# Load order, wave order, dummy matmuls and a wider handover at the start of an attention block

## The chip, the cores and the metric

The kernel runs on one core of one Trainium2 chip. The metric is the time of one execution on the device in microseconds (us). The profile gives the span from the first to the last instruction on the core; it reads about 1.7 us less than the timed figure (863.2 against 864.9 for the same execution of the kernel before).

## The reference

Two residual blocks follow each other. In both, layernorm comes first and has no learned scale.

```python
# x: 2048 x 1024, H = 32 heads of 32
qkv = layernorm(x) @ wqkv                # 1024 -> 3 x 1024
pq, pk = phi(q), phi(k)                  # phi(t) = (t + 1 if t > 0 else exp(t)) + 1e-6
kv = einsum("bhsd,bhse->bhde", pk, v)    # summed over all 2048 tokens
z  = einsum("bhsd->bhd", pk)
o  = (pq @ kv) / (pq . z + 1e-6)
h  = x + o @ wo
gate, up = layernorm(h) @ W_gate, layernorm(h) @ W_up   # 1024 -> 3584
out = h + (relu(gate) * up) @ W_down                    # 3584 -> 1024
```

`kv` and `z` need all tokens, so K and V are made for all 2048 tokens before the first output of the attention can be made. Q needs only the normalised x.

## The kernel before

The kernel is a list of operations in program order. A planner derives the semaphore waits from what each operation reads and writes. Each engine, and the one DMA-issuing queue (SP), runs its own operations in that order. Tokens are cut into 16 tiles of 128. For each tile:

- `ln1(st)`: DVE takes statistics of x (two instructions and an aggregate), POOL makes the reciprocal deviation and the shift in three tiny instructions, DVE normalises into `xn` (two buffers), and the next x tile is loaded.
- `T1(st)`: TensorE transposes `xn` in eight 128x128 blocks, ACT evicts all eight to `xnT`.
- `kvp(st)`: four pieces (K low, K high, V low, V high), eight 128x512 matmuls each; K pieces go through `phi` (an exp on ACT, two instructions on DVE).
- `kvacc(st)`: sixteen small matmuls accumulate kv and z in three PSUM banks.

```python
def T1(st):
    (b,) = alloc_banks(P1_POOL)                       # least recently used bank
    transpose8(xn[:, st % 2, :], [B_xn[st % 2]], b, NDC, "T1_%d" % st)
    evac_T("act", b, NDC, xnT[:, :, st * P:(st + 1) * P], [B_xnT[st]], "evT1_%d" % st)

# (cut) load queue at the start: NKV = 4 weight pieces of 1 MB, x tiles of 256 KB
load_x1(0, split=True)
load_wkv(0)
load_x1(1)
for nt in range(1, NKV):
    load_wkv(nt)
for st in range(2, NX1):                              # x tiles 2 and 3
    load_x1(st)

# (cut) the KV stage: tile order
ln1(0); ln1(1); T1(0)
for st in range(NST):                                 # 16 tiles
    if st + 1 < NST: T1(st + 1)
    if st + 2 < NST: ln1(st + 2)
    if st >= 1: trickle(2)                            # two later weight loads
    kvp(st)
    if st >= 1: kvacc(st - 1)
kvacc(NST - 1)
kvfin()                                               # DVE evicts kv and z

# (cut) handover to the Q projection and the attention output
for ct in range(NG): a1(0, ct, ALL)                   # 8 Q units of 8 matmuls
rest = [(sb_, ct) for sb_ in range(1, NSB) for ct in range(NG)]   # 24 more
# chain: a2 (numerators, denominators), a3 (transpose), a4 (output projection),
# a5 (second layernorm's transpose); Q units of `rest` are the filler between them
```

After that come the gated layers in four rounds. They are 75% of the time and the change does not touch them.

## Time and profile before

The time before is 864.83 us (three runs, 864.65 to 865.26). The profile page says at once what kind of kernel this is. From it, the engines' busy time (part 1: us, share of the span, instructions) and the line of part 4, which follows back the chain that ended last:

```profile
PE 841.5 (97%) x4520; PEld 406.2 (47%) x4608; DVE 275.1 (32%) x517; ACT 174.2 (20%) x258; POOL 35.1 (4%) x107
...
PE 94%; DVE 2%; DMA 1%; issue 1%; SPq 1%; ACT 1%; POOL 0%; ACTq 0%; DVEq 0%
```

TensorE is busy 97% of the span, so only its idle time and its slow time can be won by a change of order. The page alone does not say where those are. TensorE's waits do (columns: who waited, for whom, us in total, how often, longest):

```profile
PE ps L456 <- DVE xn L496: 10.8, 3, 6.5
PE ps L446 <- DVE RB L511: 1.2, 1, 1.2
PE ps L446 <- DVE kvm L572: 0.9, 1, 0.9
PE ps L456 <- ACT RE L547: 0.7, 1, 0.7
PE ps L446 <- DVE E2t L508: 0.5, 1, 0.5
```

The instants come from TensorE's timeline (start in us, duration, operation, count, and in brackets the idle time before it and what ended it). The groups are merged, so I show the lines around the waits:

```profile
6.52 1.01 PE L456 MATMUL ps<-ident,xn 128*128 128x128 bf16 x8 [6.52 <-DVE xn L496]
11.44 1.03 PE L456 MATMUL ps<-ident,xn 128*128 128x128 bf16 x8 [3.91 <-DVE xn L496]
12.27 8.45 PE L446 MATMUL ps<-RB,RA 128*128 128x512 bf16 x32
21.40 0.61 PE L456 MATMUL ps<-ident,xn 128*128 128x128 bf16 x8 [0.68 <-ACT RE L547]
22.46 6.85 PE L446 MATMUL ps<-RB,RA 128*128 128x512 bf16 x31 [0.46 <-DVE E2t L508]
...
143.03 13.76 PE L446 MATMUL ps<-RA,RC 128*128 128x512 bf16 x62 [0.88 <-DVE kvm L572]
...
158.59 0.23 PE L446 MATMUL ps<-kvm,RB 128*128 128x128 bf16 x1 [1.25 <-DVE RB L511]
```

Three things are to be read there. First, nothing useful runs before 6.52 us, the second transposes start at 11.44, and the first KV matmul at 12.27. Second, about 1.1 us are lost between 20.7 and 22.5. Third, at the handover the first Q unit waits 0.88 us for DVE's `kvm` eviction and the last of the first numerators wait 1.25 us for the last `phi`.

The group at 12.27 has a property that the merged line hides: 32 matmuls took 8.45 us, while 31 took 6.85 us at 22.46. In the single records the first seven start 0.43 us apart, the rest 0.216. (Some matmul records are missing from each trace, which is why a group of 32 can read 31.)

The reason for the first gap is on DVE (same columns):

```profile
7.94 1.29 DVE L476 BATCH_NORM_STATS2 st<-RE 128x6 f32<-128x512 bf16 x2 [1.56 <-DMA RE<-in_A_x_dram]
...
17.74 1.29 DVE L476 BATCH_NORM_STATS2 st<-RE 128x6 f32<-128x512 bf16 x2 [6.35 <-DMA RE<-in_A_x_dram]
```

The statistics of tile 1 waited 1.56 us for its x tile, which stood behind a 1 MB weight piece; those of tile 2 waited 6.35 us for an x tile that stood behind 4 MB of weights.

| what is lost before | us | where read |
|---|---|---|
| idle before the first transposes | 6.5 | waits |
| idle between first and second transposes | 3.9 | timeline, 11.44 |
| half-rate matmuls after 12.27 (7 x 0.2) | 1.4 | spacing of single records |
| idle at 21 to 22.5 | 1.1 | timeline |
| handover: kvm eviction, last phi | 0.9 + 1.25 | timeline, 143.03 and 158.59 |

### The profile page before, as it was taken

What the parts mean: (1) busy time and instruction counts of PE and PEld (TensorE: products, weight loads), DVE (VectorE), ACT (ScalarE), POOL (GpSimd) and SP (SyncE); (2) the same over time, 40 slices, a digit from 0 to 9 for tenths busy, and PEclk for the clock granted to TensorE, in tenths of its full rate; (3) what the DMA queues carried; (4) which work ended last, traced back from release to release, by engine and by line L of the source; (5) the groups of instructions that cost most, each with busy time, mean ns of one, the idle gap of its engine ahead of it and who ended that gap; (6) DMA issues with size and microseconds to landing.
All of it is one profiled execution on the core that took longest, in us unless ns stands there. A gap on an engine that the chain in (4) does not pass through costs nothing.

```text
span 863.2 us, 10884 instructions
## 1 busy us (share of the span) xinstructions
PE 841.5 (97%) x4520; PEld 406.2 (47%) x4608; DVE 275.1 (32%) x517; ACT 174.2 (20%) x258; POOL 35.1 (4%) x107
## 2 busy tenths in 40 slices
PE   4999999999999999999999999999999999999998
PEld 2555554444544444445444444454444444444443
DVE  3545434766534321115432101343411012112111
ACT  2444443332322211002222100022221001111100
POOL 2111100000000000000000000000000000000000
PEclk9999999999999999999999999999999999999999
DMA  8873000000144336553333555334254654363052
GB/s 267 266 230 128 13 1 1 2 12 29 36 144 160 110 113 206 172 171 120 122 110 122 183 186 180 122 99 141 97 178 136 205 171 156 112 195 98 25 174 93
DMA packets 105536, 109.75 MB, mean 127 GB/s; under 512 B 2960, under 2 KB 101520, under 8 KB 105488
## 3 DMA queue, kind: packets, MB, share of 16 engines
q1 hardware_dynamic: 105488, 109.06, 39.2%
q8 instruction: 36, 0.59, 0.3%
q14 instruction: 12, 0.10, 0.0%
HBM read 104.86 MB, written 4.19 MB: 126 GB/s over the span
## 4 chain that ended last, share of the span: by engine, by line
PE 94%; DVE 2%; DMA 1%; issue 1%; SPq 1%; ACT 1%; POOL 0%; ACTq 0%; DVEq 0%
PE ps L446 92%; PE ps L456 2%; DMA RE<-in_A_x_dram 1%; SPq L374 1%; DVE RB L511 1%; ACT Et L506 1%; DVE E2t L508 0%; DVE st L476 0%; DVE kvm L572 0%; DVE zc L578 0%; POOL rstd L484 0%; DVE RC L699 0%; DVE hsb L642 0%; DVE xn L496 0%; POOL nmr L487 0%
## 5 line engine op out<-in xcount | busy, mean ns | idle before, releaser
L446 PE MATMUL ps<-RE,gring 128*128 128x512 bf16 x876 | 197.2, 379 | 1.1
L446 PE MATMUL ps<-RC,gring 128*128 128x512 bf16 x877 | 195.0, 379 | 1.0
L446 PE MATMUL ps<-wdring,RA 128*128 128x512 bf16 x877 | 193.0, 379 | 1.0
L674 DVE TENSOR_TENSOR RA<-RC,ps 128x512 bf16<-128x512 bf16 x112 | 77.0, 687 | 262.0 <-PE ps L446 262.0
L672 ACT ACTIVATE RC<-ps 128x512 bf16<-128x512 f32 x112 | 67.0, 598 | 461.8 <-PE ps L446 461.8
L446 PEld LDWEIGHTS ps<-wdring,RA 128*128 128x128 bf16 x896 | 87.7, 98 | 105.7
L446 PEld LDWEIGHTS ps<-RC,gring 128*128 128x128 bf16 x896 | 87.0, 98 | 102.9
L446 PEld LDWEIGHTS ps<-RE,gring 128*128 128x128 bf16 x896 | 86.4, 98 | 100.1
L446 PE MATMUL ps<-RB,RA 128*128 128x512 bf16 x497 | 111.4, 382 | 1.2 <-DVE E2t L508 0.5
L446 PEld LDWEIGHTS ps<-RB,RA 128*128 128x128 bf16 x512 | 49.8, 99 | 58.0 <-issue 1.8
L699 DVE TENSOR_TENSOR RC<-ps,hsb 128x512 bf16<-128x512 f32 x32 | 20.2, 685 | 176.9 <-PE ps L446 176.9
L446 PE MATMUL ps<-wo,RE 128*128 128x512 bf16 x250 | 57.6, 379 | 0.3
L446 PE MATMUL ps<-RA,RC 128*128 128x512 bf16 x247 | 56.4, 379 | 1.3 <-DVE kvm L572 0.9
L506 ACT ACTIVATE Et<-ps 128x512 bf16<-128x512 f32 x64 | 38.2, 597 | 85.3 <-PE ps L446 49.2
L446 PEld LDWEIGHTS ps<-wo,RE 128*128 128x128 bf16 x256 | 25.1, 98 | 30.2
L446 PEld LDWEIGHTS ps<-RA,RC 128*128 128x128 bf16 x256 | 24.3, 98 | 27.9 <-DVE kvm L572 0.8
L508 DVE TENSOR_SCALAR E2t<-Et 128x512 bf16<-128x512 bf16 x64 | 18.7, 292 | 57.0 <-ACT Et L506 57.0
L456 PE MATMUL ps<-ident,xn 128*128 128x128 bf16 x256 | 20.3, 224 | 11.4 <-DVE xn L496 10.8
L642 DVE TENSOR_TENSOR hsb<-ps,x 128x512 bf16<-128x512 f32 x32 | 22.1, 692 | 28.9 <-PE ps L446 28.6
L481 POOL TENSOR_SCALAR ve<-mv 128x1 f32<-128x1 f32 x32 | 7.1, 223 | 579.4 <-DVE mv L479 579.4
L464 ACT ACTIVATE RE<-ps 128x1024 bf16<-128x1024 bf16 x24 | 24.5, 1022 | 24.7 <-PE ps L456 24.7
L547 ACT ACTIVATE RE<-ps 128x512 bf16<-128x512 f32 x32 | 19.1, 597 | 35.4 <-PE ps L446 35.4
(45 smaller groups left out, 323.4 us busy)
## 6 DMA issues: line engine op xcount, KB each, us to landing
gring<-in_B_W_gate_dram SPq DMA_DIRECT2D x28, 1024.0 KB, 5.3
gring<-in_B_W_up_dram SPq DMA_DIRECT2D x28, 1024.0 KB, 7.1
wdring<-in_B_W_down_dram SPq DMA_DIRECT2D x56, 512.0 KB, 3.4
RB<-in_A_wqkv_dram SPq DMA_DIRECT2D x4, 1024.0 KB, 9.5
x<-in_A_x_dram SPq DMA_DIRECT2D x16, 256.0 KB, 2.7
out_dram<-RC SPq DMA_DIRECT2D x32, 128.0 KB, 3.6
RE<-in_A_x_dram SPq DMA_DIRECT2D x15, 256.0 KB, 2.7
RC<-in_A_wqkv_dram SPq DMA_DIRECT2D x2, 1024.0 KB, 6.6
```

Of the source, the lines that this page charges most:

```text
L374: return PL.add("sp", lambda e: e.dma_start(dst_ap, src_ap), writes=wbufs, slot=slot, name=name)
L446: lambda e: e.matmul(out_ap, lhsT, rhs, start=start, stop=stop, skip_group_check=skip),
L456: lambda e, i=i: e.transpose(tb[:, i, :], src_ap[:, i * P:(i + 1) * P], ident[:]),
L464: PL.add("act", lambda e: e.activation(out=dst_ap, in_=src, func=ACTF.Identity), reads=[B_bank[b]], writes=dst_bufs, name=name)
L506: PL.add("act", lambda e: e.activation(out=Et[:, k, 0:w], in_=src, func=ACTF.Exp), reads=[B_bank[b]], writes=[B_E[k]], name=name + "_exp")
L508: PL.add("dve", lambda e: e.tensor_scalar(out=E2t[:, k, 0:w], in0=Et[:, k, 0:w], scalar1=1.0, scalar2=1e-6, op0=ALU.min, op1=ALU.add), rea ...
L511: PL.add("dve", lambda e: e.scalar_tensor_tensor(out=dst_ap, in0=src, scalar=C1, in1=E2t[:, k, 0:w], op0=ALU.add, op1=ALU.max), reads=[B_b ...
L547: PL.add("act", lambda e, b=b, j=j: e.activation(out=vv[:, slot, j * NW:(j + 1) * NW], in_=bank(b, NW), func=ACTF.Identity), reads=[B_bank ...
L642: PL.add("dve", lambda e, b=b, nt=nt: e.tensor_tensor(out=hsb[:, hs, j, nt * NW:(nt + 1) * NW], in0=bank(b, NW), in1=x2[:, xs, nt * NW:(nt ...
L672: PL.add("act", lambda e: e.activation(out=rg[:, k, :], in_=bank(ga, SBW), func=ACTF.Relu), reads=[B_bank[ga]], writes=[B_rg[k]], name="rg ...
L674: PL.add("dve", lambda e: e.tensor_tensor(out=hhT[:, ft, :], in0=rg[:, k, :], in1=bank(gb, SBW), op=ALU.mult), reads=[B_rg[k], B_bank[gb]] ...
L699: PL.add("dve", lambda e, j=j, k=k: e.tensor_tensor(out=outst[:, k, :], in0=bank(banks4[j], NW), in1=hsb[:, hs, j, dh * NW:(dh + 1) * NW], ...
```

## The change

The intent: give TensorE dense work earlier, and hide the two waits at the handover. It has six parts.

1. Load order: x tiles 0 and 1 first, then weight piece 0, x tiles 2 and 3, then pieces 1 to 3.
2. Wave order: the first four tiles are multiplied with weight piece 0 first, then all four with piece 1, and so on, so that the work starts with one piece of weights. This needs five buffers for K and V in place of three.
3. Layernorm split into statistics and norm, so that the statistics of the next tile stand on DVE right behind a norm, ahead of the `phi`.
4. In the first wave, transposes are evicted in two halves, so that the matmuls can start after the first.
5. Dummy matmuls on zeros: 14 at the start, 5 after the first transposes, to bring the array to its full rate.
6. Handover: the three KV banks are marked as just used, so the next Q unit takes another bank; two more Q units run before the first numerators.

The diff is condensed: guards for other shapes are left out, and so are the lines that only rename or split helper functions, share memory between buffers, or place the small exp that warms ACT.

```diff
-        NPK = 3
+        NPK = 5
...
+        PL.add("pool", lambda e: e.memset(zeros_t[:], 0.0), writes=[B_zeros], name="zeros")
...
+        def pe_dummies(n):
+            (b,) = alloc_banks(P1_POOL)
+            for _ in range(n):
+                mm(bank(b, 512), zeros_t[:, 0:P], zeros_t[:, 0:512], True, True, [B_zeros], B_bank[b], "dummy")
...  (T1 with split=True: two ACT evictions of half the blocks each)
         def kvfin():
+            for b_ in KVB + [BZ]:
+                touch_bank(b_)
...
         load_x1(0, split=True)
+        load_x1(1)
         load_wkv(0)
-        load_x1(1)
-        for nt in range(1, NKV):
-            load_wkv(nt)
         for st in range(2, NX1):
             load_x1(st)
+        load_wkv(1)                     # pieces 2 and 3 are queued after norm 0 and norm 1
...
-        ln1(0); ln1(1); T1(0)
-        for st in range(NST):  ...      # tile order
+        pe_dummies(14)
+        ln1_stats(0); ln1_norm(0); ln1_stats(1)
+        for st in range(4):
+            T1(st, split=True)
+            if st == 0: pe_dummies(5)
+            ln1_norm(st + 1)
+            ln1_stats(st + 2)
+            kvp_piece(st, 0)
+        for nt in range(1, NKV):
+            for st in range(4):
+                kvp_piece(st, nt)
+                if nt == NKV - 1 and st >= 1: kvacc(st - 1)
+            ...                         # T1(4) and layernorm of tiles 5, 6 after nt == 1
+        for st in range(4, NST):  ...   # tile order from here on
...
         rest = [(sb_, ct) for sb_ in range(1, NSB) for ct in range(NG)]
+        for _ in range(2):
+            sb_, ct = rest.pop(0)
+            a1(sb_, ct, ALL)
```

More of the change, by code (lines that the diff above doesn't have):

```diff
@@ L226, in bass_sequential_preLN__linear_attn_block__glu_gated_reglu__prompt_kernel @@
         hnT = [hnT0, hnT1]
-        hsb = sb("hsb", [P, 2, STB, D], bf16)
+        RF = sb("RF", [P, max(2 * STB * D, 1024)], bf16)
+        hsb = RF[:, 0:2 * STB * D].rearrange("p (a b c) -> p a b c", a=2, b=STB)
+        zeros_t = RF[:, 0:512]
+        ip_i = RF[:, 512:768].bitcast(dt.int32)
+        jp_i = RF[:, 768:1024].bitcast(dt.int32)
         xn = sb("xn", [P, 2, D], bf16)
@@ L241, in bass_sequential_preLN__linear_attn_block__glu_gated_reglu__prompt_kernel @@
         warm = sb("warm", [P, 8], f32)
-        ip_i = sb("ip_i", [P, P], dt.int32)
-        jp_i = sb("jp_i", [P, P], dt.int32)
         st6 = sb("st6", [P, NSTAT, NBC * 6], f32)
@@ L284, in bass_sequential_preLN__linear_attn_block__glu_gated_reglu__prompt_kernel @@
         B_xn = bufs("xn_", 2)
-        B_xnT = bufs("xnT_", NST)
+        B_xnT = [bufs("xnT%d_" % s_, 2) for s_ in range(NST)]
         B_wkv = bufs("wkv_", NKV)
@@ L319, in bass_sequential_preLN__linear_attn_block__glu_gated_reglu__prompt_kernel @@
         B_warm = _Buf("warm")
+        B_zeros = _Buf("zeros")
         B_ipi = _Buf("ipi")
@@ L369, in bass_sequential_preLN__linear_attn_block__glu_gated_reglu__prompt_kernel, with act_warm, dma_load @@
         PL.add("pool", lambda e: e.memset(warm[:], 0.0), writes=[B_warm], name="warm0")
-        PL.add("act", lambda e: e.activation(out=warm[:, 4:8], in_=warm[:, 0:4], func=ACTF.Exp),
-               reads=[B_warm], writes=[B_warm], name="warm_act")
-        def dma_load(slot, dst_ap, src_ap, wbufs, name):
-            return PL.add("sp", lambda e: e.dma_start(dst_ap, src_ap), writes=wbufs, slot=slot, name=name)
+        def act_warm():
+            PL.add("act", lambda e: e.activation(out=warm[:, 4:8], in_=warm[:, 0:4], func=ACTF.Exp),
+                   reads=[B_warm], writes=[B_warm], name="warm_act")
+        def dma_load(slot, dst_ap, src_ap, wbufs, name, q="sp"):
+            return PL.add(q, lambda e: e.dma_start(dst_ap, src_ap), writes=wbufs, slot=slot, name=name)
         def load_x1(st, split=False):
@@ L383, in load_x1, with load_wkv @@
                 dma_load(sl_x1[i], x1[:, i, :], xv[st * P:(st + 1) * P, :], B_x1[i], "ld_x1_%d" % st)
-        def load_wkv(nt):
+        def load_wkv(nt, q="sp"):
             dma_load(sl_wkv[nt], wkv[:, :, nt * NW:(nt + 1) * NW],
-                     wqkv_v[:, :, D + nt * NW:D + (nt + 1) * NW], [B_wkv[nt]], "ld_wkv_%d" % nt)
+                     wqkv_v[:, :, D + nt * NW:D + (nt + 1) * NW], [B_wkv[nt]], "ld_wkv_%d" % nt, q=q)
         def load_wq(i):
@@ L470, in bass_sequential_preLN__linear_attn_block__glu_gated_reglu__prompt_kernel, with layernorm @@
         stat_ctr = [0]
-        def layernorm(src_full, src_chunk_bufs, dst_ap, dst_buf, norm_eng, name):
+        def layernorm(src_full, src_chunk_bufs, dst_ap, dst_buf, norm_eng, name, defer=False):
             k = stat_ctr[0] % NSTAT
@@ L490, in layernorm, with norm @@
                    reads=[B_mv[k], B_rstd[k]], writes=[B_nmr[k]], name=name + "_nmr")
-            if norm_eng == "act":
-                PL.add("act", lambda e: e.activation(out=dst_ap, in_=src_full, func=ACTF.Identity,
-                                                     scale=rstd[:, k, :], bias=nmr[:, k, :]),
-                       reads=list(src_chunk_bufs) + [B_rstd[k], B_nmr[k]], writes=[dst_buf], name=name + "_norm")
-            else:
-                PL.add("dve", lambda e: e.tensor_scalar(out=dst_ap, in0=src_full, scalar1=rstd[:, k, :],
-                                                        scalar2=nmr[:, k, :], op0=ALU.mult, op1=ALU.add),
-                       reads=list(src_chunk_bufs) + [B_rstd[k], B_nmr[k]], writes=[dst_buf], name=name + "_norm")
+            def norm():
+                if norm_eng == "act":
+                    PL.add("act", lambda e: e.activation(out=dst_ap, in_=src_full, func=ACTF.Identity,
+                                                         scale=rstd[:, k, :], bias=nmr[:, k, :]),
+                           reads=list(src_chunk_bufs) + [B_rstd[k], B_nmr[k]], writes=[dst_buf],
+                           name=name + "_norm")
+                else:
+                    PL.add("dve", lambda e: e.tensor_scalar(out=dst_ap, in0=src_full, scalar1=rstd[:, k, :],
+                                                            scalar2=nmr[:, k, :], op0=ALU.mult, op1=ALU.add),
+                           reads=list(src_chunk_bufs) + [B_rstd[k], B_nmr[k]], writes=[dst_buf],
+                           name=name + "_norm")
+            if defer:
+                return norm
+            norm()
+            return None
         phi_ctr = [0]
@@ L523, in kv_out, with ln1_stats, ln1_norm @@
             return ps[:, KVB[col // 512], (col % 512):(col % 512) + P]
-        def ln1(st):
+        ln1_norms = {}
+        def ln1_stats(st):
             i = st % NX1
-            layernorm(x1[:, i, :], B_x1[i], xn[:, st % 2, :], B_xn[st % 2], "dve", "ln1_%d" % st)
+            ln1_norms[st] = layernorm(x1[:, i, :], B_x1[i], xn[:, st % 2, :], B_xn[st % 2], "dve",
+                                      "ln1_%d" % st, defer=True)
+        def ln1_norm(st):
+            ln1_norms.pop(st)()
             if st + NX1 < NST:
@@ L529, in ln1, with T1 @@
                 load_x1(st + NX1)
-        def T1(st):
+        def ln1(st):
+            ln1_stats(st)
+            ln1_norm(st)
+        HDC = max(1, NDC // 2)
+        def T1(st, split=False):
             (b,) = alloc_banks(P1_POOL)
             transpose8(xn[:, st % 2, :], [B_xn[st % 2]], b, NDC, "T1_%d" % st)
-            evac_T("act", b, NDC, xnT[:, :, st * P:(st + 1) * P], [B_xnT[st]], "evT1_%d" % st)
+            if split and NDC >= 2:
+                src_ = bank_bf(b)
+                PL.add("act", lambda e: e.activation(out=xnT[:, 0:HDC, st * P:(st + 1) * P], in_=src_[:, 0:HDC, :],
+                                                     func=ACTF.Identity),
+                       reads=[B_bank[b]], writes=[B_xnT[st][0]], name="evT1a_%d" % st)
+                PL.add("act", lambda e: e.activation(out=xnT[:, HDC:NDC, st * P:(st + 1) * P],
+                                                     in_=src_[:, HDC:NDC, :], func=ACTF.Identity),
+                       reads=[B_bank[b]], writes=[B_xnT[st][1]], name="evT1b_%d" % st)
+            else:
+                evac_T("act", b, NDC, xnT[:, :, st * P:(st + 1) * P], B_xnT[st], "evT1_%d" % st)
@@ new lines, in xnT_buf, with kvp_piece @@
+        def xnT_buf(st, dc):
+            return B_xnT[st][0 if dc < HDC else 1]
+        def pe_dummies(n):
+            if n <= 0:
+                return
+            (b,) = alloc_banks(P1_POOL)
+            for _ in range(n):
+                mm(bank(b, 512), zeros_t[:, 0:P], zeros_t[:, 0:512], True, True, [B_zeros], B_bank[b], "dummy")
+        def kvp_piece(st, nt):
+            slot = st % NPK
+            (b,) = alloc_banks(P1_POOL)
+            for dc in range(NDC):
+                mm(bank(b, NW), xnT[:, dc, st * P:(st + 1) * P], wkv[:, dc, nt * NW:(nt + 1) * NW],
+                   dc == 0, dc == NDC - 1, [xnT_buf(st, dc), B_wkv[nt]], B_bank[b], "kvp_%d_%d" % (st, nt))
+            if nt < ND2:
+                phi(b, NW, pk[:, slot, nt * NW:(nt + 1) * NW], B_pk[slot][nt], "k_%d_%d" % (st, nt))
+            else:
+                j = nt - ND2
+                PL.add("act", lambda e, b=b, j=j: e.activation(out=vv[:, slot, j * NW:(j + 1) * NW],
+                                                               in_=bank(b, NW), func=ACTF.Identity),
+                       reads=[B_bank[b]], writes=[B_v[slot][j]], name="v_%d_%d" % (st, j))
@@ L536, in kvp @@
         def kvp(st):
-            slot = st % NPK
             for nt in range(NKV):
-                (b,) = alloc_banks(P1_POOL)
-                for dc in range(NDC):
-                    mm(bank(b, NW), xnT[:, dc, st * P:(st + 1) * P], wkv[:, dc, nt * NW:(nt + 1) * NW],
-                       dc == 0, dc == NDC - 1, [B_xnT[st], B_wkv[nt]], B_bank[b], "kvp_%d_%d" % (st, nt))
-                if nt < ND2:
-                    phi(b, NW, pk[:, slot, nt * NW:(nt + 1) * NW], B_pk[slot][nt], "k_%d_%d" % (st, nt))
-                else:
-                    j = nt - ND2
-                    PL.add("act", lambda e, b=b, j=j: e.activation(out=vv[:, slot, j * NW:(j + 1) * NW],
-                                                                   in_=bank(b, NW), func=ACTF.Identity),
-                           reads=[B_bank[b]], writes=[B_v[slot][j]], name="v_%d_%d" % (st, j))
+                kvp_piece(st, nt)
@@ L585, in a1 @@
                 mm(bank(b, SBW), wq[:, dc, ct * P:(ct + 1) * P], xnT[:, dc, sb_ * SBW:(sb_ + 1) * SBW],
-                   dc == 0, dc == NDC - 1, [B_wq[(ct * P) // NW]] + B_xnT[sb_ * STB:(sb_ + 1) * STB],
+                   dc == 0, dc == NDC - 1,
+                   [B_wq[(ct * P) // NW]] + [xnT_buf(s_, dc) for s_ in range(sb_ * STB, (sb_ + 1) * STB)],
                    B_bank[b], "a1_%d_%d" % (sb_, ct))
@@ L723, in d_round @@
                     d_evac(j)
+        WB = min(4, NST)
         load_x1(0, split=True)
-        load_wkv(0)
         if NST > 1:
             load_x1(1)
-        for nt in range(1, NKV):
-            load_wkv(nt)
+        load_wkv(0)
+        act_warm()
         for st in range(2, min(NX1, NST)):
             load_x1(st)
+        if NKV > 1:
+            load_wkv(1)
+        late_wkv = list(range(2, NKV))
         bulk = []
@@ L750, in trickle @@
                     bulk.pop(0)()
-        ln1(0)
-        if NST > 1:
-            ln1(1)
-        T1(0)
-        for st in range(NST):
+        NDUM0, NDUM1 = 14, 5
+        pe_dummies(NDUM0)
+        ln1_stats(0)
+        ln1_norm(0)
+        if late_wkv:
+            load_wkv(late_wkv.pop(0))
+        if NST > 1:
+            ln1_stats(1)
+        for st in range(WB):
+            T1(st, split=True)
+            if st == 0:
+                pe_dummies(NDUM1)
+            if st + 1 < NST:
+                ln1_norm(st + 1)
+            if st == 0:
+                while late_wkv:
+                    load_wkv(late_wkv.pop(0))
+            if st + 2 < NST:
+                ln1_stats(st + 2)
+            kvp_piece(st, 0)
+        while late_wkv:
+            load_wkv(late_wkv.pop(0))
+        for nt in range(1, NKV):
+            for st in range(WB):
+                kvp_piece(st, nt)
+                if nt == NKV - 1 and st >= 1:
+                    kvacc(st - 1)
+            if nt == 1:
+                if WB < NST:
+                    T1(WB)
+                if WB + 1 < NST:
+                    ln1_norm(WB + 1)
+                if WB + 2 < NST:
+                    ln1_stats(WB + 2)
+        for st in range(WB, NST):
             if st + 1 < NST:
@@ L759, in bass_sequential_preLN__linear_attn_block__glu_gated_reglu__prompt_kernel @@
             if st + 2 < NST:
-                ln1(st + 2)
-            if st >= 1:
-                trickle(2)
+                ln1_norm(st + 2)
+            if st + 3 < NST:
+                ln1_stats(st + 3)
+            trickle(2)
             kvp(st)
-            if st >= 1:
-                kvacc(st - 1)
+            kvacc(st - 1)
         kvacc(NST - 1)
@@ L773, in bass_sequential_preLN__linear_attn_block__glu_gated_reglu__prompt_kernel @@
         rest = [(sb_, ct) for sb_ in range(1, NSB) for ct in range(NG)]
+        for _ in range(2):
+            if rest:
+                sb_, ct = rest.pop(0)
+                a1(sb_, ct, ALL)
         chain = [("a2", 0), ("a2", 1), ("a2", 2), ("a3", 0), ("a2", 3), ("a3", 1), ("a4", 0),
```

## The prediction

> What bounds it now. TensorE is busy 841.5 of 863.2 us (97%, page part 1); the chain that ended last is 94% TensorE. The change adds no useful matmul and removes none, so it can only win idle or half-rate TensorE time. From TensorE's waits and timeline:
> - Start: first transposes at 6.52 us (after the first layernorm), second at 11.44 (3.9 us idle: x tile 1 queued behind a 1 MB weight load, its statistics started only at 7.94), first KV matmul at 12.27. Its first seven or so start 0.43 us apart, later ones 0.216. The Trainium skill, "TensorE: Matmul & The Clock Gate", Part 1, says that an idle array runs at half rate until about 3.4 us of activity; the spacing until 15.1 us (3.7 after 11.44) agrees, although the granted-clock column reads 1.00.
> - 20.7 to 22.5: about 1.1 us idle; x tile 2 landed only at 17.7, behind 4 MB of weights.
> - Handover: 0.9 us at 142 (the first Q projection waits for the bank that the kvm eviction reads) and 1.25 us at 157 (the first numerators wait for the last phi).
> The rest (0.3 us at 217, about 4 at the end, missing records) is untouched.
>
> What changes. x tiles 0 and 1 load before the weights, so the statistics of tile 1 follow norm 0 directly. The first wave (four token tiles against weight piece 0) needs one 1 MB piece; pieces 1, 2, 3 follow. Fourteen dummy matmuls (from about 1.3 us, 0.43 us each cold) lift the clock before the first transposes at about 6.6; they end near 6.2 to 7.3. The zeros memset on POOL delays the index setup and DVE by some 0.3 us.
>
> In the first wave transposes are no longer prefetched: each tile pays transpose 0.5, half eviction about 0.8 with latency, eight matmuls 1.73: 3.0 us. The layernorm chain is longer: statistics 1.29, aggregate 0.21, three POOL steps with latencies 1.4, norm 0.55: about 3.45 us from norm to norm. So norms end near 6.7, 10.1, 13.6, 17.0; first KV matmul near 9, fourth transposes near 17.1, end of wave 0 near 20.1. From there TensorE should be dense: piece 1 lands near 12 us, 2 and 3 near 17 and 21 (350 GB/s in the DMA view), needed at 20, 27, 34.
>
> Sum. Before, at 22.46 us TensorE had done 4 KV pieces and 3 transposes. After, at about 20.1, 4 and 4 (a transpose tile is worth 0.66 us). Gain 2.4 + 0.66 = about 3.0 us. At the handover the bank touch and two extra Q units remove 0.9 + 1.25 = 2.1 us. All of it is on the critical path. Together 5.1 us: 864.8 - 5.1 = 859.7 us, 0.6%. Range 857.0 to 862.5. Chances: faster by over 2% 0.01, within 2% 0.98, slower by over 2% 0.01.
>
> What would show it. First KV matmul at 8.5 to 9.5 us; first-wave matmuls spaced 0.216 from the start; gaps of 0.7 to 1.3 us per tile between 11 and 18 us released by half eviction and norm; no wait over 0.3 us from 20 to 157; the waits for kvm and the last phi gone; after that every stage shifted as a block.
>
> What would make it wrong. Dummies running past 7 us, or the array falling back to half rate in the first wave, where it is busy only about 65%: 1 to 3 us lost. A phi on DVE ahead of the next norm, lengthening the chain. A new wait for weight pieces 2 or 3, queued behind x loads that wait for norms. Fewer Q units late in the chain, exposing layernorm 2. Or a tighter chain: 2 us more.

## More of the kernel before

Where I compare stages I use profiled spans and instants, because the trace resolves tenths of a microsecond; where I compare whole kernels I also give the timed runs.

## The result, and the profile after

The changed kernel takes 859.81 us (median of ten runs, 859.76 to 859.97); the kernel before, timed beside it, 865.04 (twelve runs). The ratio is 0.994, with a 95% interval of 0.993 to 0.9949. Ratios here are the mean time of one kernel's runs over that of the other's runs of the same rounds, so they are not quite the ratio of the medians. The change wins 5.2 us, 0.6%.

The same lines of the page:

```profile
PE 845.6 (99%) x4538; PEld 407.2 (47%) x4627; DVE 273.3 (32%) x517; ACT 174.0 (20%) x262; POOL 35.4 (4%) x108
...
PE 96%; DVE 2%; issue 1%; POOL 1%; ACT 0%; DVEq 0%; ACTq 0%; POOLq 0%
```

TensorE is busy 4.1 us more, in a span 5.2 us shorter. Part of that is the 19 dummies, which count as busy: a busy share that rises is no proof of more useful work. TensorE's waits:

```profile
PE ps L451 <- ACT RA L562: 2.1, 3, 0.7
PE ps L451 <- POOL RF L344: 1.4, 1, 1.4
PE ps L461 <- DVE xn L504: 0.8, 2, 0.5
```

What is left are three waits of 0.7 us for ACT's half evictions, the start, and two short ones for a norm. The waits for `kvm` and for the last `phi` are gone. TensorE's timeline:

```profile
1.37 4.95 PE L451 MATMUL ps<-RF 128*128 128x512 bf16 x14 [1.37 <-POOL RF L344]
...
8.30 1.89 PE L451 MATMUL ps<-RB,RA 128*128 128x512 bf16 x8
10.04 0.62 PE L461 MATMUL ps<-ident,xn 128*128 128x128 bf16 x8
11.37 1.90 PE L451 MATMUL ps<-RB,RA 128*128 128x512 bf16 x7 [0.71 <-ACT RA L562]
13.38 0.62 PE L461 MATMUL ps<-ident,xn 128*128 128x128 bf16 x8
...
16.73 0.62 PE L461 MATMUL ps<-ident,xn 128*128 128x128 bf16 x8
18.04 8.81 PE L451 MATMUL ps<-RB,RA 128*128 128x512 bf16 x39 [0.69 <-ACT RA L562]
...
139.31 10.74 PE L451 MATMUL ps<-RA,RC 128*128 128x512 bf16 x49
```

The first KV matmuls start at 8.30 us. Between 10 and 18 us one tile takes 3.35 us: transposes at 10.04, 13.38, 16.73. From 18.04 on TensorE is dense. The period is set on DVE, which the norm lines of its timeline show:

```profile
6.08 0.55 DVE L504 TENSOR_SCALAR xn<-RE,rstd,nmr 128x1024 bf16<-128x1024 bf16 x1 [1.37 <-POOL nmr L492]
...
9.43 0.55 DVE L504 TENSOR_SCALAR xn<-RE,rstd,nmr 128x1024 bf16<-128x1024 bf16 x1 [1.36 <-POOL nmr L492]
...
12.78 0.55 DVE L504 TENSOR_SCALAR xn<-RE,rstd,nmr 128x1024 bf16<-128x1024 bf16 x1 [0.48 <-POOL nmr L492]
```

The norms start at 6.08, 9.43, 12.78 and 16.12, each after POOL's last small result. Per tile DVE runs 1.28 us of statistics, 0.21 of aggregate and 0.55 of norm (which overlaps the next instruction by about 0.1), and between aggregate and norm lies POOL's chain of three instructions on 128x1 values, about 1.36 us of waiting. The four sum to 3.40 us, less the overlap. At 12.78 the line shows only 0.48 us of idle time before the norm, because the `phi` of the piece before was done inside POOL's wait.

To see where the 5.2 us came from, I mark two instants in every trace: the start of the last matmul of the KV accumulation, and the start of the first gate matmul.

| trace | last KV accumulate | from there to first gate matmul | from there to the end | span |
|---|---|---|---|---|
| before | 141.99 | 77.94 | 643.2 | 863.2 |
| after | 139.07 | 75.73 | 643.2 | 858.0 |
| difference | -2.92 | -2.21 | 0.0 | -5.1 |

The start wins 2.92 us, the handover 2.21, and the gated layers shift as a block. That the sum came out does not yet say which of the six parts earned it.

### The profile page after: what moved, and what is told of

The parts are those of the page before. It is cut to its first block, busy times and chain, and to the rows that moved or that the text cites. A ratio compares the mean times of both kernels' runs of the same rounds, so it can differ in the third digit from the quotient of the medians.

```text
span 858.0 us, 10919 instructions
## 1 busy us (share of the span) xinstructions
PE 845.6 (99%) x4538; PEld 407.2 (47%) x4627; DVE 273.3 (32%) x517; ACT 174.0 (20%) x262; POOL 35.4 (4%) x108
## 4 chain that ended last, share of the span: by engine, by line
PE 96%; DVE 2%; issue 1%; POOL 1%; ACT 0%; DVEq 0%; ACTq 0%; POOLq 0%
PE ps L451 94%; PE ps L461 2%; DVE st L481 1%; POOL rstd L489 0%; DVE xn L504 0%; POOL nmr L492 0%; POOL ve L486 0%; DVE mv L484 0%; DVE RE L525 0%; DVE RF L693 0%; DVE RC L750 0%; ACT Et L520 0%; ACT RA L562 0%; POOL RF L344 0%; DVE RF L360 0%
## 5 line engine op out<-in xcount | busy, mean ns | idle before, releaser
L750 DVE TENSOR_TENSOR RC<-ps,RF 128x512 bf16<-128x512 f32 x32 | 20.2, 685 | 176.9 <-PE ps L451 176.9
L693 DVE TENSOR_TENSOR RF<-ps,x 128x512 bf16<-128x512 f32 x32 | 22.1, 691 | 28.7 <-PE ps L451 28.6
L591 ACT ACTIVATE RE<-ps 128x512 bf16<-128x512 f32 x32 | 19.1, 597 | 36.3 <-PE ps L451 36.3
L525 DVE SCALAR_TENSOR_TENSOR RE<-ps,E2t 128x512 bf16<-128x512 f32 x32 | 22.1, 692 | 1.1
```

The source lines that it names most:

```text
L525: PL.add("dve", lambda e: e.scalar_tensor_tensor(out=dst_ap, in0=src, scalar=C1, in1=E2t[:, k, 0:w], op0=ALU.add, op1=ALU.max), reads=[B_b ...
L591: PL.add("act", lambda e, b=b, j=j: e.activation(out=vv[:, slot, j * NW:(j + 1) * NW], in_=bank(b, NW), func=ACTF.Identity), reads=[B_bank ...
L693: PL.add("dve", lambda e, b=b, nt=nt: e.tensor_tensor(out=hsb[:, hs, j, nt * NW:(nt + 1) * NW], in0=bank(b, NW), in1=x2[:, xs, nt * NW:(nt ...
L750: PL.add("dve", lambda e, j=j, k=k: e.tensor_tensor(out=outst[:, k, :], in0=bank(banks4[j], NW), in1=hsb[:, hs, j, dh * NW:(dh + 1) * NW], ...
```

## The experiments

Two views were to be told apart. In one, each part of the change has a worth of its own, and the load order is most of the 3.0 us at the start; this was my working theory at first. In the other, the start is a race between three suppliers of TensorE (the load queue, the layernorm chain, the rate of the array), and a part pays only where its supplier is the slowest. All twelve kernels gave the correct result. They ran in three batches of four, each batch on a chip of its own with the kernel before timed beside (medians 864.92, 865.16 and 865.06); the changed kernel had been timed in a run before that.

| kernel | timed median (range) | ratio to before | span | last KV accumulate | handover stage |
|---|---|---|---|---|---|
| before | 865.04 (864.65 to 865.54) | 1 | 863.2 | 141.99 | 77.94 |
| after | 859.81 (859.76 to 859.97) | 0.994 | 858.0 | 139.07 | 75.73 |
| a_nodum | 861.45 (860.98 to 862.10) | 0.9956 | 859.7 | 140.75 | 75.73 |
| a_nomid | 859.83 (859.79 to 861.48) | 0.9941 | 858.1 | 139.09 | 75.73 |
| b_loads | 863.80 (863.31 to 864.11) | 0.9982 | 861.9 | 140.72 | 77.94 |
| b_hand | 862.78 (862.52 to 862.82) | 0.9971 | 860.8 | 141.84 | 75.73 |
| a_notouch | 860.58 (860.57 to 860.83) | 0.995 | 858.9 | 139.08 | 76.53 |
| a_nounits | 861.16 (861.16 to 861.17) | 0.9956 | 859.4 | 139.07 | 77.13 |
| a_nosplit | 861.12 (860.84 to 861.32) | 0.9955 | 859.6 | 140.61 | 75.73 |
| a_stats2 | 859.07 (858.68 to 859.83) | 0.9933 | 857.3 | 138.28 | 75.73 |
| b_loads_hand | 861.33 (860.92 to 861.63) | 0.9957 | 859.2 | 140.22 | 75.73 |
| b_loads_hand_dum | 861.22 (860.95 to 862.21) | 0.9957 | 859.5 | 140.55 | 75.73 |
| a_oldloads | 871.18 (869.18 to 871.94) | 1.0064 | 869.5 | 150.49 | 75.73 |
| a_stats3 | 857.07 (856.61 to 857.36) | 0.9907 | 854.9 | 135.91 | 75.73 |

"a_" kernels are the changed kernel with one edit, "b_" kernels the kernel before with one or more parts of the change. The ratios' 95% intervals reach 0.001 to 0.002 to each side (some 0.9 to 1.5 us). Smaller steps rest on the traces: the two columns on the right come from one profiled execution each. How far single executions differ can be seen where an edit leaves the start alone: b_hand's KV stage ends 0.15 us earlier than that of the kernel before, and b_loads_hand's 0.5 us earlier than b_loads'.

### The handover: b_hand, a_notouch, a_nounits

b_hand puts both handover edits into the kernel before and nothing else.

```diff
# b_hand: kernel before plus
+            for b_ in KVB + [BZ]:
+                touch_bank(b_)
+        for _ in range(2):
+            if rest:
+                sb_, ct = rest.pop(0)
+                a1(sb_, ct, ALL)
# a_notouch: changed kernel without the first two of these lines
# a_nounits: changed kernel without the last four
```

> The kernel before with the two handover edits alone: the three KV accumulator banks are marked as just used, and two more Q units run ahead of the first numerators. Theory: the waits of 0.88 and 1.25 us vanish and nothing comes back later: span 861.0 to 861.2, 2.1 us less. Rival (the next chain step takes it back, since fewer Q units are left as filler): less than 1 us, with a new wait of TensorE between 157 and 220 us.

> The changed kernel without the marking of the three KV banks as just used. Theory: the first Q unit again takes a bank that the kvm eviction still reads; a wait of about 0.9 us behind DVE at the handover; span 858.9. Rival (the two extra Q units or the new bank history already avoid it): no wait, span 858.0.

> The changed kernel without the two Q units ahead of the first numerators. Theory: the first numerators again wait about 1.25 us for the last phi on DVE; span 859.3. Rival: other order of banks and DVE work hides it, span 858.0 to 858.3.

Measured: b_hand won 2.1 us of timed median (862.78 against 864.92), and its handover stage is 75.73 us, exactly the changed kernel's, against 77.94 before. (b_hand's span, 860.8, lies 0.2 below the range given, because the KV stage of that execution ended 0.15 us early.) Without the bank mark the stage is 0.80 us longer, without the two units 1.40, together 2.20. The waits come back, the first one somewhat shorter (0.7 us against 0.88). From TensorE's waits, first in a_notouch, then in a_nounits:

```profile
PE ps L451 <- DVE kvm L620: 0.7, 1, 0.7
```
```profile
PE ps L451 <- DVE RB L525: 1.2, 1, 1.2
```

So this part of the prediction is shown by removing and by adding it: the handover is worth 2.2 us, it is the sum of two separate waits, and nothing is given back later although fewer Q units are left as filler.

### The dummies: a_nodum, a_nomid

```diff
# a_nodum
-        NDUM0, NDUM1 = 14, 5
+        NDUM0, NDUM1 = 0, 0
# a_nomid
-        NDUM0, NDUM1 = 14, 5
+        NDUM0, NDUM1 = 14, 0
```

> The changed kernel without any dummy matmul. Theory (the dummies matter): the first transposes and the first KV piece run at half rate (0.107 and 0.43 us apart instead of 0.054 and 0.216), which costs 0.4 + 1.7 us and perhaps a second half-rate piece; the last matmul of the first wave moves from 19.77 us to 21.5 to 23.5, and the profiled span from 858.0 to about 860 to 861.5. Rival (the layernorm chain of 3.35 us per tile sets the wave, so the rate doesn't matter): the chain catches up, span within 0.3 us of 858.0.

> The changed kernel with the 14 dummies at the start but without the 5 between the first transposes and the first KV piece. Theory: the five only fill the 0.8 us in which the first eviction is awaited, and the array keeps its full rate over so short a pause; the first KV piece starts about 0.2 us earlier, the second transposes still wait for the second norm at 9.98; span within 0.2 us of 858.0. Rival (the pause drops the rate): spacing 0.43 us in the first piece, span up by 1 us or more.

Measured: without any dummy the KV stage ends 1.68 us later and the timed median is 1.6 us higher. The end of wave 0 is near 21.7 us, in the range I gave; the span, 859.7, just missed its lower edge of 860. TensorE's timeline of a_nodum:

```profile
6.78 1.01 PE L461 MATMUL ps<-ident,xn 128*128 128x128 bf16 x8 [6.78 <-DVE xn L504]
8.83 3.55 PE L451 MATMUL ps<-RB,RA 128*128 128x512 bf16 x8 [1.04 <-DMA RB<-in_A_wqkv_dram]
```

The eight transposes took 1.01 us instead of 0.61, and the first eight KV matmuls 3.55 us instead of 1.89: spacing 0.107 and 0.43 us, half the rate. By 12.22 the array was at full rate. The Trainium skill's page "TensorE: Matmul & The Clock Gate", Part 1, describes this: an idle array is gated to half its clock until it has seen about 3.4 us of activity, in a window that runs freely and does not start with the kernel. The trace agrees: the last slow matmul starts at 11.79 and the transposes at 12.22 are fast, so that the rate rose 3.0 to 3.4 us after the dense work began at 8.83. The free-running window shows too. In the profile of the changed kernel the dummies begin at 1.37 and the spacing falls to 0.216 at 5.07, which is 3.7 us later; in a_nosplit, begun at 1.36, all fourteen dummies are at half rate, until 6.89, which is 5.5 us. One wave piece was slow, not two, and part of that was recovered: without the dummies the following tiles came 3.08 us apart (13.56, 16.64), faster than the layernorm chain's 3.35, because TensorE was late and the norms of these tiles ended 0.5 to 0.8 us before it came to them.

About 0.4 us of the 1.68 are not the rate's: weight piece 0 landed at 8.79 us in this execution (7.67 in the changed kernel's), and TensorE waited for it from the end of the first half eviction, 8.43, to 8.83. The five runs lie 1.2 to 2.3 us above the changed kernel.

The five dummies in the middle are worth nothing in the trace: a_nomid's KV stage ends at 139.09, and its median is 859.83. The first piece did not start earlier, as I had expected, because in that run weight piece 0 had landed later and TensorE waited for it. One of a_nomid's five runs took 861.48 us. No trace was taken of that one. Its mean granted clock is 0.999 (1.000 in the other four), which would fit a short fall of the rate, but 0.999 also stands beside runs that were not slow (860.58 us in a_notouch). Whether the pause had lowered the rate there, which the five dummies are meant to prevent, stays open.

### The load order alone: b_loads

```diff
# b_loads: kernel before, load queue only
         load_x1(0, split=True)
-        load_wkv(0)
         if NST > 1:
             load_x1(1)
-        for nt in range(1, NKV):
-            load_wkv(nt)
+        load_wkv(0)
         for st in range(2, min(NX1, NST)):
             load_x1(st)
+        for nt in range(1, NKV):
+            load_wkv(nt)
```

> The kernel before with one edit: the loads of x tiles 1, 2 and 3 are queued before weight pieces 0 and 1 to 3 as in the change; no wave order, no split, no dummies, no handover edit. Theory (most of the 3.0 us won at the start comes from the load order): second transposes at about 10.0 instead of 11.44 us, no wait for x tile 2 at 20.7, the second tile's KV pieces start at about 19.9 to 20.3 instead of 22.46, span 860.6 to 861.0 (2.2 to 2.6 us less than 863.2), limited by weight piece 3 landing near 18. Rival (the wave order and the dummies win it): less than 1 us, span 862.2 or more.

Measured: both expectations missed. The KV stage ends 1.27 us earlier (span 861.9, timed 1.1 us less), which is between the two. In b_loads_hand below, with the same load order, it ended 1.77 us earlier, because there the first layernorm and the weight pieces came 0.4 to 0.5 us sooner; so the load order is worth 1.1 to 1.8 us. The waits moved as they should: tile 1's transposes start at 10.27 instead of 11.44 and no wait for x tile 2 is left. But a new wait appeared. From TensorE's waits of b_loads:

```profile
PE ps L446 <- DMA RB<-in_A_wqkv_dram: 0.9, 1, 0.9
```

In tile order the first tile needs all four weight pieces within 8 us. The two x tiles now stand ahead of pieces 1 to 3, so piece 3 lands at 18.75 instead of 17.04 us, and the last KV piece of tile 0 starts at 18.79 after a wait of 0.86 us. The Trainium skill's page "DMA: Bandwidth & Descriptors", section "Two DMAs through the same engine are not ordered", says that descriptors within one queue of one DMA engine start in order, and that nothing orders transfers across the 16 engines. Here the order held for whole loads: in all fourteen traces the loads of the first 20 us landed in the order in which they were queued (in b_loads x tile 3 at 9.76 us, pieces 1 to 3 at 12.76, 15.78 and 18.75). So what is moved ahead in the queue is paid for by everything behind it, here 0.5 MB at about 350 GB/s, some 1.5 us.

### The parts together: b_loads_hand, b_loads_hand_dum

```diff
# b_loads_hand: b_loads plus b_hand
# b_loads_hand_dum: the same plus
+        pe_dummies(14)
         ln1(0)
         ln1(1)
         T1(0)
+        pe_dummies(12)
```

> The kernel before with the load order and the two handover edits together; tile order, no dummies, no split. From the runs so far: load order alone 861.9, handover alone 860.8, before 863.2. Theory (the two add up, being on different stretches of one dense TensorE chain): 863.2 - 1.3 - 2.3 = 859.6, range 859.3 to 860.0, which is the span of the changed kernel without dummies (859.7), so that the wave order without dummies would be worth nothing over the load order. Rival (they overlap): 860.5 or more.

> The same with dummy matmuls: 14 at the start and 12 between the first and second transposes, which keep the array at full rate. Theory (in tile order the first tile's four KV pieces are bound by the landing of weight piece 3 near 18.8 us, so a faster array only waits longer): span within 0.3 us of the same kernel without dummies; longer waits of TensorE behind weight loads. Rival (dummies are worth their 1.7 us in any order): span about 858.

Measured: 861.33 us without dummies, 861.22 with them, both 0.9957 of before; profiled spans 859.2 and 859.5. The load order and the handover add up, as expected (the span lies 0.1 below the range given). The dummies did their work and won nothing. TensorE's timeline of b_loads_hand_dum:

```profile
12.62 1.90 PE L449 MATMUL ps<-RB,RA 128*128 128x512 bf16 x8 [0.46 <-DMA RB<-in_A_wqkv_dram]
15.62 1.90 PE L449 MATMUL ps<-RB,RA 128*128 128x512 bf16 x8 [1.10 <-DMA RB<-in_A_wqkv_dram]
18.62 1.90 PE L449 MATMUL ps<-RB,RA 128*128 128x512 bf16 x8 [1.10 <-DMA RB<-in_A_wqkv_dram]
```

The first piece runs at full rate, and then each following piece waits for its weights: 0.46, 1.10 and 1.10 us. The pieces land 3.0 us apart and are used up in 1.73 us. A faster array only waits longer.

Now four kernels with the same handover stand side by side. Tile order without dummies 861.33, tile order with dummies 861.22, wave order without dummies 861.45, wave order with dummies 859.81. Neither the wave nor the dummies is worth anything measurable alone on top of the load order; together they are worth about 1.5 us. Here "wave" stands for three of the six parts: both kernels with the wave order also have the split layernorm and the half evictions. Without the half evictions the pair wins next to nothing (a_nosplit below, 861.12); the split layernorm was not tested alone. The reasons are in the traces: in tile order the weight loads bind, so the rate does not matter; in wave order without dummies the half-rate piece binds, so the early start does not matter. The view in which each part has a worth of its own falls for these two parts. It holds for the handover, which lies on another stretch of the chain.

### The wave without the load order: a_oldloads

```diff
# a_oldloads: changed kernel, load queue of before
         load_x1(0, split=True)
-        load_x1(1)
         load_wkv(0)
-        for st in range(2, min(NX1, NST)):
-            load_x1(st)
-        if NKV > 1:
-            load_wkv(1)
-        late_wkv = list(range(2, NKV))
+        load_x1(1)
+        for nt in range(1, NKV):
+            load_wkv(nt)
+        for st in range(2, min(NX1, NST)):
+            load_x1(st)
+        late_wkv = []
```

> The changed kernel with the old load queue (x 0, weight piece 0, x 1, pieces 1 to 3, then x 2 and 3). Theory (the wave needs x tiles early as tile order needs weights early): x tiles 2 and 3 land near 17.7 and 18.4, the norm of tile 2 ends near 21.3, of tile 3 near 24.6, wave 0 ends near 27.5 instead of 19.8; span 865 to 866, slower than before. Rival (load order is a small term): less than 2 us over 858.0.

Measured: 871.18 us, slower than before by 6 us and than the changed kernel by 11. The direction is as expected, the size is not. TensorE's timeline:

```profile
12.96 0.62 PE L461 MATMUL ps<-ident,xn 128*128 128x128 bf16 x8 [2.29 <-DVE xn L504]
...
22.65 1.03 PE L461 MATMUL ps<-ident,xn 128*128 128x128 bf16 x8 [5.38 <-DVE xn L504]
24.38 3.59 PE L451 MATMUL ps<-RB,RA 128*128 128x512 bf16 x8 [0.69 <-ACT RA L562]
```

The wait of 5.38 us at 22.65 is the expected one (x tile 2 landed at 19.1, later than I had taken it). But eight KV matmuls at 24.38 took 3.59 us: the array had fallen back to half rate. The windows view of the same kernel (stretch and its length, busy time and count of PE, PEld, DVE, ACT, POOL, then granted clock, DMA share, GB/s) shows it:

```profile
12.00:16.00 4.00, 2.35 (x14) 1.21 (x15) 0.55 (x1) 1.08 (x2) 0.27 (x1) 0.86 1.11 350
...
24.00:28.00 4.00, 3.62 (x11) 1.40 (x12) 2.83 (x7) 0.81 (x2) 1.51 (x5) 0.50 0.38 115
```

The granted clock went to half at 14.91 us, inside the first of these stretches and before the long wait, and came back at 28.56. It had first risen at 4.67; the changes are 10.24 and 13.65 us apart, three and four times 3.41, so that they fall on a grid of 3.41 us. In the 3.4 us before 14.91 TensorE had worked about 1.3 us (0.6 of them transposes), and the longest idle stretch was 2.3 us, from 10.67 to 12.96. The excess over the 865.5 us that I had expected adds up: x tile 2 landed 1.4 us later than assumed, and the eight KV matmuls and sixteen transposes at half rate between 22.65 and 28.5 cost about 8 x 0.21 + 16 x 0.05 = 2.5 us, together 3.9 of 4.0. The other runs fit: two of the five took 869.2 and 869.3 us, with a mean granted clock of 0.996 in place of 0.992, which by my estimate from these figures is some 7 us at half rate in place of 14. So the wave order without the load order is harmful. It needs four x tiles early, as tile order needs four weight pieces early, and with the idle time comes the half rate.

### The eviction in halves: a_nosplit

```diff
-            T1(st, split=True)
+            T1(st)
```

> The changed kernel with the transposes of the first wave evicted by one instruction (1.02 us) in place of two halves (0.60 each, of which the second overlaps the matmuls). Theory: TensorE waits 0.42 us longer per tile; tiles 1 to 3 then take 0.45 + 1.3 + 1.73 = 3.5 us against a layernorm chain of 3.35, so the wave ends 0.6 to 1.0 us later, span 858.6 to 859.0. Rival (the chain alone sets the wave, only the last tile's wait shows): span 858.4.

Measured: span 859.6 and 861.12 timed, 1.3 us above the changed kernel, more than I expected. In TensorE's waits, against 2.1 us for ACT in the changed kernel:

```profile
PE ps L451 <- ACT RA L469: 3.5, 3, 1.2
```

The tiles come 3.50 us apart (transposes at 10.80, 14.30, 17.81), so the loop through TensorE and ACT is now longer than the layernorm chain. That has a second effect which I had left out: the changed kernel's wave hides a late start of the first tile behind the layernorm chain, while here nothing hides it, and in this execution the dummies had ended late (the first transposes at 7.26). Of the 1.54 us by which the KV stage ends later, 0.76 is there already at the second transposes, 0.32 comes from two periods, and 0.46 from the last eviction.

### The layernorm chain: a_stats2, a_stats3

If the chain of 3.35 us per tile sets the wave, then it can be cut: DVE works only about 2.9 us per tile (1.28 + 0.21 + 0.5 for the layernorm, 0.9 for the `phi` of the K piece), the rest is waiting for POOL. a_stats2 takes statistics of two tiles before the norm of the first, transposes one tile ahead, and uses pieces with weight piece 1 as filler.

```diff
# a_stats2: changed kernel, first wave rewritten (cut)
-        for st in range(WB):
-            T1(st, split=True)
-            ...
+        ln1_stats(0); ln1_stats(1); ln1_norm(0)
+        T1(0, split=True); pe_dummies(4)
+        ln1_norm(1); ln1_stats(2)
+        T1(1, split=True)
+        kvp_piece(0, 0)
+        ln1_stats(3); ln1_norm(2)
+        kvp_piece(1, 0)
+        T1(2, split=True); ln1_norm(3)
+        kvp_piece(0, 1)
+        T1(3, split=True); ln1_stats(4)
+        kvp_piece(2, 0); kvp_piece(1, 1); kvp_piece(3, 0); ln1_norm(4)
+        kvp_piece(2, 1); kvp_piece(3, 1); ln1_stats(5); T1(4); ln1_norm(5); ln1_stats(6)
```

> The changed kernel with a reordered first wave: statistics of tile 1 ahead of norm 0, of tile 3 ahead of norm 2 (so the three POOL steps of one tile run under the statistics of the next), transposes one tile ahead, and KV pieces of weight piece 1 as filler. Theory (the layernorm chain's latency of 3.35 us per tile, not DVE's busy time of about 2.9 us and not the loads, sets the end of the first wave): TensorE dense from about 12.5 us, the waits of 0.7 us behind ACT gone, span 855 to 856. Rival (the loads or DVE throughput set it): a new wait for weight piece 1 (landing at 12.0) or for a norm, span 857.5 or more.

Measured: 859.07 us, span 857.3, so the expected 855 to 856 was missed. The timeline of all engines shows why:

```profile
11.44 0.26 POOL L492 TENSOR_SCALAR nmr<-mv,rstd 128x1 f32<-128x1 f32 x1
...
12.02 0.69 DVE L525 SCALAR_TENSOR_TENSOR RE<-ps,E2t 128x512 bf16<-128x512 f32 x1
12.63 1.28 DVE L481 BATCH_NORM_STATS2 st<-RE 128x6 f32<-128x512 bf16 x2
...
14.07 0.49 DVE L504 TENSOR_SCALAR xn<-RE,rstd,nmr 128x1024 bf16<-128x1024 bf16 x1
...
14.62 0.56 PE L461 MATMUL ps<-ident,xn 128*128 128x128 bf16 x7 [1.87 <-DVE xn L504]
```

POOL's last result for tile 2 started at 11.44. The norm that needs it started at 14.07, because in DVE's program order it stood behind the `phi` of the first KV piece (12.02) and the statistics of tile 3 (12.63). The Trainium skill's page "TensorE: Matmul & The Clock Gate", Part 1, gives the queues of ScalarE and VectorE as strict FIFO; this trace agrees, with 2.4 us in which a ready norm did not run and 1.87 us in which TensorE waited for it. a_stats3 moves three operations: the statistics of tile 3 and the norm of tile 2 go ahead of the first `phi`, the norm of tile 3 ahead of the second.

```diff
# a_stats3 against a_stats2
         ln1_norm(1); ln1_stats(2)
+        ln1_stats(3)
         T1(1, split=True)
+        ln1_norm(2)
         kvp_piece(0, 0)
-        ln1_stats(3); ln1_norm(2)
+        ln1_norm(3)
         kvp_piece(1, 0)
-        T1(2, split=True); ln1_norm(3)
+        T1(2, split=True)
```

> The reordered first wave again with one mend: in the run before, the norm of tile 2 was ready at 11.7 us but stood on DVE behind the phi of the first KV piece and the statistics of tile 3, and ended at 14.6, a wait of 1.87 us for TensorE. Now statistics 2 and 3 and norm 2 go ahead of that phi. Theory: norm 2 ends near 12.4, TensorE dense from 8.7 us on, span 855.2 to 855.6. Rival (DVE is simply full there, or weight piece 1, landing near 12.5, binds): 856.5 or more.

Measured: 857.07 us (856.61 to 857.36), span 854.9, a little under the range given (the profiled run was the fastest of the four; the others' spans are 855.1 to 855.6); the ratio to before is 0.9907 with an interval of 0.9894 to 0.9921. Its whole list of TensorE's waits, and its timeline:

```profile
PE ps L451 <- POOL RF L344: 1.4, 1, 1.4
PE ps L461 <- DVE xn L504: 0.3, 1, 0.3
```

```profile
8.36 0.62 PE L461 MATMUL ps<-ident,xn 128*128 128x128 bf16 x8
8.81 3.40 PE L451 MATMUL ps<-RB,RA 128*128 128x512 bf16 x15
...
14.89 8.80 PE L451 MATMUL ps<-RB,RA 128*128 128x512 bf16 x39
```

TensorE is dense from 8.36 us on: the waits for ACT and for the norms at the start are gone, and only the old 0.3 us at the second layernorm is left. The KV stage ends 3.16 us earlier than in the changed kernel. This kernel beats both: 8.0 us less than the kernel before in the medians of its own call, and 2.7 us less than the changed kernel, though those two were timed in different calls.

## Why the prediction was right

The prediction said 859.7 us, and 859.81 was measured. Point by point:

- What bounds the kernel (TensorE's own order, idle and half-rate time only): right. From the first gate matmul to the end, both kernels take 643.2 us.
- The start is worth 3.0 us: measured 2.92. That the sum came so close is partly luck. Its first term, 2.4 us (22.46 to 20.1), came out as 2.7 (22.46 to 19.77), and its second, 0.66 for the transposes done ahead, as only 0.2 (what the two KV stages still take after these instants, 119.53 and 119.30 us); the two errors cancelled. The prediction put the norms' ends near 6.7, 10.1, 13.6 and 17.0; they ended at 6.6, 10.0, 13.3 and 16.7, 3.35 us apart rather than 3.45. The fourth transposes came at 16.73 (17.1 predicted), the end of wave 0 at 19.8 (20.1). The first KV matmul was earlier than the range given, 8.30 against 8.5 to 9.5, without effect, since the chain of norms sets the wave.
- The handover is worth 2.1 us: measured 2.21, as 0.80 and 1.40, and shown on its own in b_hand.
- Weight pieces 1 to 3 were put at 12, 17 and 21 us; they landed at 12.0, 15.7 and 19.4, and no wait was seen.
- The gaps per tile: 0.7 us, at the lower edge of the 0.7 to 1.3 given, released by the half eviction. The prediction named the norm as the other releaser, and it is: norms 2 and 3 ended at 13.33 and 16.67 and the transposes began at 13.38 and 16.73. The waits view books nothing for this, because the modelled end of the matmuls before reaches to 13.27 and 16.6.
- Dummies past 7 us were named as a risk of 1 to 3 us. In a_notouch they ran that long (the fourteenth started at 6.88) and the KV stage still ended at 139.08. The layernorm chain absorbs it. The risk was real only where that chain is not the longest, as in a_nosplit.
- The fall back to half rate was named as a risk for a wave in which the array is busy only about 65%. The trace of the changed kernel shows about 75% (2.52 us of the 3.35 from 13.38), and no fall. It did happen in a_oldloads, at a lower share.

What the prediction did not do is say which part earns the 3.0 us. My working theory after it, that the load order is most of it, failed at b_loads: alone it gave 1.27, since I had not counted what the x tiles ahead of them cost the weight pieces. The wave and the dummies add the rest only as a pair. A side effect that I had not predicted is steadiness: the changed kernel's ten runs lie within 0.21 us, while those of a_nodum spread over 1.1 and those of b_loads_hand over 0.7. I take this to be the same absorption: a chain on DVE that does not depend on the array's window or on the last 0.5 us of a load sets the pace. In favour of it, a_notouch and a_nounits, which keep the wave, also stay within 0.26 and 0.01 us; against it stands the one longer run of a_nomid. It is an argument from the spreads; no run tested it by itself.

## What to carry to other kernels

At the start of a kernel, list the suppliers of the main engine (load queue, preparation chain, the array's rate) with the time at which each could have it running, and change the latest first; an edit to another shows nothing, and two edits may pay only together. Reordering a load queue only moves the wait to whatever was pushed back, so compare the need times of all loads behind it. On an engine that runs strictly in order, a long chain with gaps is cut by placing ready work of the next tile into the gap, and an operation that others wait for goes ahead of those that nobody waits for.

## What the Trainium skill lacked or had wrong

- "TensorE: Matmul & The Clock Gate", Part 1, gives an idle window of about 3.4 us as what throttles a running array, and the section "HAM oscillation" an idle gap above 3.4 us; only the section "A second HAM failure mode: psum-queue depth-cycling" tells of shorter, frequent idle stretches that do it, without a figure. In a_oldloads the granted clock fell to half at 14.91 us with no idle stretch longer than 2.3 us; TensorE had been busy 1.26 us (37%) of the 3.41 us before. In b_loads_hand_dum, busy 1.90 of 3.41 us (56%) from 14.79 to 18.20 (a window counted in steps of 3.41 from its first clock record at 4.55), it did not fall. The page does not say what share of a window is enough; these two runs put it between 37 and 56%.
- No page that I read tells how a mean granted clock counts the time before the first clock record of a trace. Here it counts as full rate: the windows view reads 1.00 from 12.27 to 20 us of the kernel before, and the mean of a_nodum is 1.000, though in both the first matmuls are 0.43 us apart. The records in the packed trace begin where the spacing falls (15.05 us in the kernel before, 4.95 in the changed one), and a_nodum and b_loads have none. So the half-rate start is read from the spacing of the matmuls, or from where the records begin, and not from the mean.
- "TensorE: Matmul & The Clock Gate", Part 1, says that the ramp's penalty is under 1% of a typical kernel's span and advises against fitting a count of slow matmuls. This is not wrong here: a_nodum loses 1.6 us of 860. But it is a third of what the whole change won.
